# Sliding-window attention with a mixture of adapters: longer load runs, a new row order, and the copies that undo it

## The chip, the cores and the metric

The kernel runs on one core of one Trainium2 chip. The metric is the device time of one execution in microseconds (us). The core has five engines that run their own instruction queues in order: TensorE (PE, with its weight loads shown as PEld), VectorE (DVE), ScalarE (ACT), GpSimd (POOL) and SyncE (SP). Sixteen DMA engines move data; here POOL issues all loads and SP all stores.

## The reference

`q`, `k` and `v` have shape (8 batches, 8 heads, 576 positions, 64). Attention sees only keys within 32 positions:

```
scores = q @ k.T / sqrt(64), masked to |i - j| <= 32
attn   = softmax(scores);  x = (attn @ v), heads side by side: (4608, 512)
logits = x @ w_gate                    # 8 experts
w      = softmax over the two best experts
out    = x + sum over the two experts of w_e * (x @ A[e]) @ B[e]   # rank 16
```

Output is float32; the kernels compute in f16 with float32 accumulation.

## The kernel before

**Work units.** Two heads form a pair, so a batch has four pairs and the kernel 32 units `u` (`b, n = divmod(u, 4)`). The 576 keys of a unit are nine blocks of 64; both heads of a pair stand in one 128-row stationary operand (`kTs`, block diagonal), so one score matmul gives, for one key block, 128 rows (64 keys for each of two heads) by 128 query columns: the block's own 64 queries and 32 on either side. Eight blocks form a score tile `t` of two PSUM banks; 36 tiles run across the unit borders (4.5 tiles a batch).

**One unit.** `transposes(u, 0)` and `(u, 1)` turn q and k into `qTs` and `kTs` through a PSUM tile `tp` (pool `pt`, two buffers). `score(t)` first writes the mask with a matmul by `ident` (L182), then adds the scores (L186), and ScalarE's exponential writes them to one of four `PTs` (L191). `pv(u)` multiplies by `vbd` (L206), whose extra column of ones gives the row sums; VectorE takes the reciprocal (`rc`, L214) and scales into `xs` (`xb`, L215).

**The adapters.** One batch later, `moe_step` runs in four parts: `moe_xT` transposes `xs` (L227, L230; pool `pt` too) and `moe_zl` computes logits and all eight low-rank products (L238), a chain of small VectorE operations makes the gate, ending in `zs` (L262); `moe_zT` (L271, L274) and `moe_out` (L282, L284, L287) finish, two groups of 128 rows at a time, and SP stores (L291).

**Loads.** `load(b, w)` fetches q or k with two-row runs, three DMAs each, and `pair_heads` (L92) regroups heads on VectorE; `load_v` fetches v in sixteen DMAs of one-row runs. All go two batches ahead through POOL's queue, and cast from float32 to f16 on the way.

**Layout of rows.** Because two neighbouring positions share a partition (`j = 2`), queries and keys are held even positions first, and L187 of the kernel writes the score columns back in position order: `out=ps[:, i].rearrange("p (k j) -> p j k", j=2)`.

**Order.** The kernel's text gives an order by unit: regroup, transposes two units ahead, scores one unit ahead, the product, the adapter part of four units ago. The framework then orders the instructions on each engine at build time. PSUM tiles of `score`, `pv`, `moe_zl` and `moe_out` share one pool of three (`pw`).

Of the kernel before, what the change touches and what calls it, by code (L numbers as in the profile page):

```python
# [28 lines left out]
def kernel(  # L29
# [18 lines left out]
    NB = 9  # L48
    NG = 5
    TB = 8  # L50
    GS = 188
    VD = D + 1
    NEG = -30000.0
    NU = B * NP
    NT = NU * NB // TB

# [9 lines left out]


    NV = 3
    vbd = [const.tile([128, NP, NB, 2 * VD], F16, name=f"vbd{i}") for i in range(NV)]

    def load(b, w):
        d = load_pool.tile([96, 3, H, 2, D], F16, tag=f"l{w}", name=f"l{w}")
        src = (q, k)[w][b].rearrange("h (g p j) d -> g p h (j d)", g=3, j=2)
        for g in range(3):
            nc.gpsimd.dma_start(
                out=d[:, g].rearrange("p h j d -> p h (j d)"), in_=src[g])
        raw[b, w] = d

    def load_v(b):
        d = vbd[b % NV]  # L80
        src = v[b].rearrange("(n h) (a p j) d -> h j n p a d", h=2, p=32, j=2)
        for n in range(NP):
            for h in range(2):
                for j in range(2):
                    p0 = 64 * h + 32 * j
                    nc.gpsimd.dma_start(  # L86
                        out=d[p0:p0 + 32, n, :, VD * h:VD * h + D], in_=src[h, j, n])

    def pair_heads(b, w):
        d = cast_pool.tile([96, 3, 2, H, D], F16, tag=f"c{w}", name=f"c{w}")  # L90
        for g in range(3):
            nc.vector.tensor_copy(out=d[:, g],  # L92
                                  in_=raw[b, w][:, g].rearrange("p h j d -> p j h d"))
        qk[b, w] = d

    raw, qk = {}, {}
    load(0, 0)
    load(0, 1)

# [3 lines left out]
    for i in range(NV):  # L103
        nc.vector.memset(vbd[i], 0.0)
        nc.vector.memset(vbd[i][0:64, :, :, D], 1.0)
        nc.vector.memset(vbd[i][64:128, :, :, VD + D], 1.0)

    load_v(0)
    pair_heads(0, 0)
    pair_heads(0, 1)  # L110


    mask = const.tile([128, 4, 128], F16)
    nc.gpsimd.memset(mask, 0.0)
    for s in range(4):
        jk = s % 2
        blk = mask[32 * s:32 * s + 32]
        nc.gpsimd.affine_select(out=blk, in_=blk, compare_op=ALU.is_ge, fill=NEG,
                                base=-jk, channel_multiplier=-2,
                                pattern=[[0, 4], [1, 128]])  # L120
        nc.gpsimd.affine_select(out=blk, in_=blk, compare_op=ALU.is_ge, fill=NEG,  # L121
                                base=64 + jk, channel_multiplier=2,
                                pattern=[[0, 4], [-1, 128]])

    NQ = 4
    qTs = [const.tile([128, 2, 320], F16, name=f"qT{i}") for i in range(NQ)]
    kTs = [const.tile([128, NB, 128], F16, name=f"kT{i}") for i in range(NQ)]
    for t in qTs:
        nc.vector.memset(t[:, :, 0:16], 0.0)
        nc.vector.memset(t[:, :, 304:320], 0.0)  # L130
    for t in kTs:
        nc.vector.memset(t, 0.0)
    NPT = 4
    PTs = [const.tile([128, TB, 256], F16, name=f"PT{i}") for i in range(NPT)]
    for t in PTs:
        nc.vector.memset(t, 0.0)
# [3 lines left out]
    load_v(1)  # L140

# [13 lines left out]

    def transposes(u, which):
        b, n = divmod(u, NP)
        src = qk[b, which].rearrange("p g j h d -> p g j (h d)")
        tp = pt.tile([128, 1024], F16, tag="t", name="tp")
        for g in range(3):  # L160
            for j in range(2):
                if which == 0:
                    o = tp[:, 288 * j + 96 * g:288 * j + 96 * g + 96]
                else:
                    o = tp[:, 192 * g:192 * g + 192].rearrange(
                        "p (a j k) -> p a j k", a=3, j=2)[:, :, j]
                nc.tensor.matmul(  # L167
                    out=o, lhsT=src[:, g, j, 128 * n:128 * n + 128],
                    rhs=ident[0:96, 0:96], is_transpose=True, start=True, stop=True)
        if which == 0:  # L170
            nc.vector.tensor_copy(
                out=qTs[u % NQ][:, :, 16:304],
                in_=tp[:, 0:S].rearrange("p (j s) -> p j s", j=2))
        else:
            kt = tp[:, 0:S].rearrange("p (a k) -> p a k", k=64)
            nc.vector.tensor_copy(out=kTs[u % NQ][0:64, :, 0:64], in_=kt[0:64])  # L176
            nc.scalar.copy(out=kTs[u % NQ][64:128, :, 64:128], in_=kt[64:128])  # L177

    def score(t):
        ps = pw.tile([128, TB, 128], F32, tag="w", name="ps")  # L180
        for i in range(0, TB, 4):
            nc.tensor.matmul(out=ps[:, i:i + 4], lhsT=ident, rhs=mask,  # L182
                             start=True, stop=False)
        for i in range(TB):
            u, a = divmod(TB * t + i, NB)
            nc.tensor.matmul(  # L186
                out=ps[:, i].rearrange("p (k j) -> p j k", j=2),  # L187
                lhsT=kTs[u % NQ][:, a, :],
                rhs=qTs[u % NQ][:, :, 32 * a:32 * a + 64],
                start=False, stop=(i % 4 == 3))  # L190
        nc.scalar.activation(out=PTs[t % NPT][:, :, 64:192], in_=ps,  # L191
                             func=AF.Exp, scale=1.0 / float(D) ** 0.5)
# [3 lines left out]
    def pv(u):  # L196
# [4 lines left out]
        for g in range(NG):  # L201
            ops = [(a, off) for a, off in ((2 * g - 1, 128), (2 * g, 64), (2 * g + 1, 0))
                   if 0 <= a < NB]
            for i, (a, off) in enumerate(ops):
                t, sl = divmod(NB * u + a, TB)
                nc.tensor.matmul(  # L206
                    out=po[:, GS * g:GS * g + 2 * VD],
                    lhsT=PTs[t % NPT][:, sl, off:off + 128],
                    rhs=vbd[b % NV][:, n, a, :],
                    start=(i == 0), stop=(i == len(ops) - 1))  # L210
# [3 lines left out]
        nc.vector.reciprocal(out=rc, in_=pog[:, :, :, D])  # L214
        nc.vector.tensor_tensor(  # L215
            out=xs[b][:, :, 128 * n:128 * n + 128].rearrange("p g (h d) -> p g h d", h=2),
            in0=pog[:, :, :, 0:D], in1=bcast(rc, 3, D), op=ALU.mult)

# [58 lines left out]
    def moe_out(b, gs):  # L277
        zT = st[b, "zT"]
        n = len(gs)
        pd = pw.tile([128, 2, DD], F32, tag="w", name="pd")  # L280
        for i, g in enumerate(gs):
            nc.tensor.matmul(out=pd[:, i], lhsT=zT[:, g], rhs=B_sb,  # L282
                             start=True, stop=False)
            nc.tensor.matmul(out=pd[:, i], lhsT=ident, rhs=xs[b][:, g],  # L284
                             start=False, stop=True)
# [21 lines left out]

    for w in (0, 1):
        transposes(0, w)
    for w in (0, 1):  # L310
        transposes(1, w)
# [10 lines left out]
    for u in range(NU):  # L322
        b, n = divmod(u, NP)
        if n == 0 and b + 1 < B:
            pair_heads(b + 1, 0)
        if n == 1 and b + 1 < B:
            pair_heads(b + 1, 1)
# [4 lines left out]
        if u + 2 < NU:  # L332
            transposes(u + 2, 0)
            transposes(u + 2, 1)
# [40 lines left out]
```

## Time and profile before

| | |
|---|---|
| median of three runs | 215.91 us (215.25 to 219.85) |
| span of the profiled execution (core 0) | 211.4 us; no other time is recorded for it |
| mean granted TensorE clock | 0.936 |
| busy PE, DVE, ACT, POOL | 147.6, 119.9, 85.6, 128.3 us |
| instructions | 4124 |
| chain that ended last, by engine | PE 52%, DVE 19%, POOL 11%, ACT 9% |
| HBM read, written | 28.85 MB, 9.44 MB |
| DMA packets | 86642, of which 81888 under 512 B |

The span runs from the first to the last instruction. The page's slices divide it in 40 stretches of 5.3 us, each digit a busy share in tenths; its groups put together instructions of one line, engine and operands, with the idle time of the engine just before them and what ended it. In the list of waits the numbers are total us, count, longest. In the chain and the timeline each row is start, duration, engine, what. A mean over several pipelined matmuls overstates what one adds; the length of a run of them divided by their number does not.

### The profile page before, as it was taken

Reading aid. Unit: us, or ns where it says so; the run is one execution under the profiler, and the core shown is the slowest. Engines: PE = TensorE matmul, PEld = TensorE weight load, DVE = VectorE, ACT = ScalarE, POOL = GpSimd, SP = SyncE. Lnnn points to the kernel's source line nnn. Section 1 sums busy time; section 2 is a strip of 40 time slices with the busy share of each in tenths; the row PEclk is TensorE's granted clock in tenths of the full one; section 3 lists DMA queues with packets and bytes.
Section 4 is the critical chain, followed back from the end, with each engine's and each line's share of the span. In section 5 each row is a group of like instructions: output and inputs, shape, how many; then the busy total and the mean of one; then the engine's idle time right before and its main releaser. Section 6 shows DMA issues by size and latency. Waiting matters only on the chain.

```text
span 211.4 us, 4124 instructions
## 1 busy us (share of the span) xinstructions
PE 147.6 (70%) x1600; PEld 114.4 (54%) x1600; DVE 119.9 (57%) x337; ACT 85.6 (40%) x109; POOL 128.3 (61%) x197
## 2 busy tenths in 40 slices
PE   0030279998299949987699729964998599848481
PEld 0010158996268835876378626864687468726330
DVE  6787026668814891379346851688349734844700
ACT  2001015663357334553275144723683466246032
POOL 7999995999799469835983797699480000000000
PEclk9999999999969995999699997999999999999955
DMA  6998099999999998998999999999993023003306
GB/s 59 157 63 56 1 140 125 67 42 154 138 101 144 244 96 54 208 210 87 63 167 249 103 89 153 258 98 147 172 189 55 0 90 136 5 0 123 100 0 223
DMA packets 86642, 24.12 MB, mean 114 GB/s; under 512 B 81888, under 2 KB 82016, under 8 KB 86624
## 3 DMA queue, kind: packets, MB, share of 16 engines
q0 software_dynamic: 81376, 14.44, 86.3%
q1 hardware_dynamic: 5248, 9.44, 13.2%
q8 instruction: 12, 0.20, 0.4%
q14 instruction: 6, 0.05, 0.1%
HBM read 28.85 MB, written 9.44 MB: 181 GB/s over the span
## 4 chain that ended last, share of the span: by engine, by line
PE 52%; DVE 19%; POOL 11%; ACT 9%; issue 4%; DMA 3%; ACTq 0%; POOLq 0%
PE ps L186 13%; PE po L206 9%; PE ps L182 7%; PE pd L282 5%; PE tp L167 5%; PE pd L284 5%; POOL vbd_82 L86 4%; DVE xb L215 4%; PE pz L238 3%; DMA l_189<-in_k_dram 3%; DVE zs L262 3%; PE tx L227 3%; DVE xT L230 3%; ACT zT L274 3%; PE tz L271 2%
## 5 line engine op out<-in xcount | busy, mean ns | idle before, releaser
L86 POOL DMA_DIRECT2D vbd_83<-in_v_dram x48 | 29.3, 616 | 12.0 <-DMA vbd_83<-in_v_dram 4.8
L86 POOL DMA_DIRECT2D vbd_82<-in_v_dram x48 | 29.3, 617 | 9.0 <-DMA l_496<-in_q_dram 2.7
L182 PE MATMUL ps<-mask,ident 128*128 128x512 f16 x72 | 24.6, 423 | 12.7 <-POOL mask L121 12.0
L214 DVE RECIPROCAL rc<-po 128x10 f32<-128x10 f32 x32 | 7.0, 218 | 38.2 <-PE po L206 38.1
L287 ACT COPY obt<-pd 128x1024 f32<-128x1024 f32 (+1 forms) x24 | 20.8, 869 | 16.8 <-PE pd L284 16.0
L215 DVE TENSOR_TENSOR xb<-po,rc 128x640 f16<-128x640 f32 x32 | 26.2, 820 | 0.7
L86 POOL DMA_DIRECT2D vbd_84<-in_v_dram x32 | 19.5, 619 | 7.3 <-DMA vbd_84<-in_v_dram 2.6
L282 PE MATMUL pd<-B_sb,zT 128*128 128x512 f16 x40 | 18.3, 459 | 4.2 <-ACT zT L274 4.2
L271 PE MATMUL tz<-ident,zs 128*128 128x128 f16 x40 | 4.0, 234 | 21.0 <-DVE zs L262 21.0
L227 PE MATMUL tx<-ident,xb 128*128 128x128 f16 x160 | 14.7, 220 | 5.4 <-DVE xT L230 4.8
L284 PE MATMUL pd<-xb,ident 128*128 128x512 f16 x40 | 18.4, 461 | 0.0
L230 DVE COPY xT<-tx 128x512 f16<-128x512 f16 x40 | 15.6, 416 | 2.4 <-PE tx L227 1.6
L177 ACT COPY kT_164<-tp 64x576 f16<-64x576 f16 x8 | 5.1, 633 | 25.0 <-DVE kT_164 L176 25.0
L227 PEld LDWEIGHTS <-xb 128*128 128x128 f16 x160 | 11.3, 101 | 6.9 <-issue 4.9
L271 PEld LDWEIGHTS <-zs 128*128 128x128 f16 x40 | 2.4, 102 | 22.8 <-DVE zs L262 22.8
L182 PEld LDWEIGHTS <-ident 128*128 128x128 f16 x72 | 6.6, 110 | 14.3 <-issue 14.1
L238 PE MATMUL pz<-WA_sb,xT 128*128 128x136 f16 x160 | 13.9, 223 | 0.4 <-DVE xT L230 0.4
L186 PE MATMUL ps<-qT_160,kT_164 128*128 128x128 f16 x72 | 11.1, 317 | 2.4 <-ACT kT_164 L177 2.4
L177 ACT COPY kT_161<-tp 64x576 f16<-64x576 f16 x8 | 5.1, 634 | 18.2 <-DVE kT_161 L176 18.1
L274 ACT COPY zT<-tz 128x640 f16<-128x640 f16 x8 | 5.5, 692 | 16.6 <-PE tz L271 16.6
L191 ACT ACTIVATE PT_178<-ps 128x1024 f16<-128x1024 f32 x9 | 9.2, 1023 | 6.6 <-PE ps L186 5.7
L191 ACT ACTIVATE PT_180<-ps 128x1024 f16<-128x1024 f32 x9 | 9.2, 1023 | 6.1 <-PE ps L186 5.2
(209 smaller groups left out, 375.4 us busy)
## 6 DMA issues: line engine op xcount, KB each, us to landing
out_dram<-obt SPq DMA_DIRECT2D x24, 256.0 KB, 4.0
out_dram<-obt SPq DMA_DIRECT2D x16, 192.0 KB, 2.7
vbd_82<-in_v_dram POOLq DMA_DIRECT2D x48, 36.0 KB, 2.8
vbd_83<-in_v_dram POOLq DMA_DIRECT2D x48, 36.0 KB, 3.4
vbd_84<-in_v_dram POOLq DMA_DIRECT2D x32, 36.0 KB, 3.2
l_85<-in_q_dram POOLq DMA_DIRECT2D x3, 192.0 KB, 4.8
l_89<-in_k_dram POOLq DMA_DIRECT2D x3, 192.0 KB, 6.4
l_185<-in_q_dram POOLq DMA_DIRECT2D x3, 192.0 KB, 4.6
```

Of the source, the lines that this page charges most:

```text
L86: nc.gpsimd.dma_start(out=d[p0:p0 + 32, n, :, VD * h:VD * h + D], in_=src[h, j, n])
L182: nc.tensor.matmul(out=ps[:, i:i + 4], lhsT=ident, rhs=mask, start=True, stop=False)
L186: nc.tensor.matmul(out=ps[:, i].rearrange("p (k j) -> p j k", j=2), lhsT=kTs[u % NQ][:, a, :], rhs=qTs[u % NQ][:, :, 32 * a:32 * a + 64], ...
L191: nc.scalar.activation(out=PTs[t % NPT][:, :, 64:192], in_=ps, func=AF.Exp, scale=1.0 / float(D) ** 0.5)
L206: nc.tensor.matmul(out=po[:, GS * g:GS * g + 2 * VD], lhsT=PTs[t % NPT][:, sl, off:off + 128], rhs=vbd[b % NV][:, n, a, :], start=(i == 0) ...
L215: nc.vector.tensor_tensor(out=xs[b][:, :, 128 * n:128 * n + 128].rearrange("p g (h d) -> p g h d", h=2), in0=pog[:, :, :, 0:D], in1=bcast( ...
L227: nc.tensor.matmul(out=tp[:, 128 * c:128 * c + 128], lhsT=xs[b][:, g, 128 * c:128 * c + 128], rhs=ident, is_transpose=True, start=True, st ...
L230: nc.vector.tensor_copy(out=st[b, "xT"][:, g].rearrange("p c k -> p (c k)"), in_=tp[:, 0:512])
L238: nc.tensor.matmul(out=pz[:, GS * g:GS * g + ER + E], lhsT=xT[:, g, c, :], rhs=WA_sb[:, c, :], start=(c == 0), stop=(c == 3))
L282: nc.tensor.matmul(out=pd[:, i], lhsT=zT[:, g], rhs=B_sb, start=True, stop=False)
L284: nc.tensor.matmul(out=pd[:, i], lhsT=ident, rhs=xs[b][:, g], start=False, stop=True)
L287: nc.scalar.copy(out=ob[:, 0:n], in_=pd[:, 0:n])
```

## The change

- **Loads.** q and k come in runs of eight rows of one head, v in runs of two rows (eight DMAs). `load_v` puts both rows of a run side by side in `vbd`; `shift_v` then moves the second row to its own partitions with two VectorE copies. The head pairs are now heads `n` and `n + 4`.
- **Transposes.** A batch is transposed in three thirds of 96 partitions instead of by unit, 16 matmuls each third; `regroup` brings the two heads of a pair together first (two VectorE copies a third). `qTs` and `kTs` hold a whole batch, two buffers each. ScalarE writes all of q, undoing the eight-row order as it reads PSUM; VectorE and ScalarE write one half of k each.
- **Scores.** Query columns are now in position order, so score columns are written contiguously; only the keys are permuted.
- **Mask.** It becomes the stationary operand (`maskT`, 128 columns), the moving one is `ident` repeated four times.
- **Values.** The column of ones comes first, and the moving operand is two runs of 65.
- **Residual.** Added by four matmuls with the transposed x (`xT`) against `ident`, instead of one with `ident` against `xs`.
- **Setup.** Fewer zeros are written on VectorE; those for the second `kTs` and the second and third `vbd` go to POOL, behind the second batch's loads and ahead of the weights.

```diff
     def load(b, w):
-        d = load_pool.tile([96, 3, H, 2, D], F16, tag=f"l{w}", name=f"l{w}")
-        src = (q, k)[w][b].rearrange("h (g p j) d -> g p h (j d)", g=3, j=2)
+        d = load_pool.tile([FT, NT3, 2, J * D], F16, tag=f"l{w}", name=f"l{w}")
+        src = (q, k)[w][b].rearrange("(o n) (p j) d -> (n p) o (j d)", o=2, j=J)
...
     def load_v(b):
+        src = v[b].rearrange("(o n) (a p j two) d -> o j p (n a) (two d)",
+                             o=2, p=8, j=4, two=2)
+        for o in range(2):
+            for j in range(4):
+                p0 = 64 * o + 8 * j
+                c0 = VW * o + V0
+                nc.gpsimd.dma_start(out=d[p0:p0 + 8, :, c0:c0 + 2 * D], in_=src[o, j])
+
+    def shift_v(b):
+        d = vbd[b % NV]
+        for o in range(2):
+            p0 = 64 * o
+            c0 = VW * o + V0
+            nc.vector.tensor_copy(out=d[p0 + 32:p0 + 64, :, c0:c0 + D],
+                                  in_=d[p0:p0 + 32, :, c0 + D:c0 + 2 * D])
+
+    def regroup(b, t):
+        for w in (0, 1):
+            nc.vector.tensor_copy(
+                out=qk[b, w][:, t],
+                in_=raw[b, w][:, t].rearrange("p o (j d) -> p j o d", j=J))
...
+    maskT = const.tile([128, 2, 2, 4, 8], F16)
+    nc.gpsimd.memset(maskT, 0.0)
...
     load(1, 0)
     load(1, 1)
     load_v(1)
+    shift_v(0)
+    init_kq(1, nc.gpsimd)
+    init_v(1, nc.gpsimd)
+    init_v(2, nc.gpsimd)
...
+    def transposes(b, t):
+        for w in (0, 1):
+            src = qk[b, w].rearrange("p t j o d -> p t j (o d)")
+            tp = pt.tile([128, 1024], F16, tag="t", name="tp")
+            for j in range(J):
+                slot = j if w == 0 else 4 * (j % 2) + j // 2
                 nc.tensor.matmul(
+                    out=tp[:, FT * slot:FT * slot + FT], lhsT=src[:, t, j, :],
+                    rhs=ident[0:FT, 0:FT], is_transpose=True, start=True, stop=True)
+            if w == 0:
+                c0 = QP + J * FT * t
+                nc.scalar.copy(
+                    out=qTs[b % 2][:, c0:c0 + J * FT].rearrange("p (f j) -> p f j", j=J),
+                    in_=tp[:, 0:J * FT].rearrange("p (j f) -> p f j", j=J))
+            else:
+                kt = tp[:, 0:J * FT].rearrange("p (j a f) -> p a j f", j=J, f=8)
...
+                    if o == 0:
+                        nc.vector.tensor_copy(out=dst, in_=src_)
+                    else:
+                        nc.scalar.copy(out=dst, in_=src_)
...
-            nc.tensor.matmul(out=ps[:, i:i + 4], lhsT=ident, rhs=mask,
-                             start=True, stop=False)
+            nc.tensor.matmul(out=ps[:, i:i + 4],
+                             lhsT=maskT.rearrange("p o a j f -> p (o a j f)"),
+                             rhs=bcast(ident, 1, 4), start=True, stop=False)
...
-                out=ps[:, i].rearrange("p (k j) -> p j k", j=2),
-                lhsT=kTs[u % NQ][:, a, :],
-                rhs=qTs[u % NQ][:, :, 32 * a:32 * a + 64],
+                out=ps[:, i], lhsT=kTs[b % 2][:, NB * n + a, :],
+                rhs=qTs[b % 2][:, c0:c0 + 128],
...
-                    rhs=vbd[b % NV][:, n, a, :],
+                    rhs=rhs[:, :, V0 - 1:V0 + D],
...
-            nc.tensor.matmul(out=pd[:, i], lhsT=ident, rhs=xs[b][:, g],
-                             start=False, stop=True)
+            for c in range(4):
+                nc.tensor.matmul(out=pd[:, i, 128 * c:128 * c + 128], lhsT=xT[:, g, c],
+                                 rhs=ident, start=False, stop=(c == 3))
...
+        if n < 2 and b + 1 < B:
+            regroup(b + 1, n + 1)
+        if n == 2 and b + 1 < B:
+            shift_v(b + 1)
+        if n == 3 and b + 2 < B:
+            regroup(b + 2, 0)
+        if n < NT3 and b + 1 < B:
+            transposes(b + 1, n)
```

More of the change, by code (lines that the diff above doesn't have):

```diff
@@ L109 @@
[L109 to L123, printed above, removed]
```

134 lines of the change are left out of this document (63 added, 71 removed).

## The prediction, made before the changed kernel was run

> **What bounds the kernel now.** I read the page first: shares, the 40 slices, the DMA queues.
>
> ```profile
> span 211.4 us, 4124 instructions
> PE 147.6 (70%) x1600; PEld 114.4 (54%) x1600; DVE 119.9 (57%) x337; ACT 85.6 (40%) x109; POOL 128.3 (61%) x197
> ...
> PEclk9999999999969995999699997999999999999955
> DMA  6998099999999998998999999999993023003306
> ...
> q0 software_dynamic: 81376, 14.44, 86.3%
> ```
>
> The DMA engines look full for the first 160 us, which invites a prediction about transfers. The waits decide whether that counts:
>
> ```profile
> DVE rc L214 <- PE po L206: 38.1, 24, 4.4
> PE tz L271 <- DVE zs L262: 21.0, 8, 3.3
> PE ps L182 <- POOL mask L121: 12.0, 1, 12.0
> DVE c_275 L92 <- DMA l_185<-in_q_dram: 10.7, 3, 8.6
> ```
>
> The one long DMA wait of a compute engine (c_275) is at the start; later loads run two batches ahead and only POOL, which issues them, waits for landings. So DMA does not set the steady pace. What recurs is PE waiting for `zs` and VectorE waiting for PE. I therefore cut the batch in two stages, in two successive periods, at `zs` (gated z) and at the `rc` of the batch's fourth head pair (call it C):
>
> ```profile
> 124.67 0.82 DVE L262 TENSOR_TENSOR zs<-pz,gate 128x640 f16<-128x640 f32 x1
> 134.95 0.22 DVE L214 RECIPROCAL rc<-po 128x10 f32<-128x10 f32 x1 [1.50 <-PE po L206]
> 146.84 0.82 DVE L262 TENSOR_TENSOR zs<-pz,gate 128x640 f16<-128x640 f32 x1
> 157.08 0.22 DVE L214 RECIPROCAL rc<-po 128x10 f32<-128x10 f32 x1 [2.80 <-PE po L206]
> 164.01 0.20 DVE L248 TENSOR_REDUCE m_2246<-pz 128x5 f32<-128x40 f32 x1 [0.18 <-PE pz L238]
> 167.33 0.82 DVE L262 TENSOR_TENSOR zs<-pz,gate 128x640 f16<-128x640 f32 x1
> ```
>
> Stage 1, C to end of `zs` (the next batch's first pair D, x transposes, gate), took 12.7 and 11.1 us: VectorE's stage. Stage 2, end of `zs` to next C, took 9.5 and 9.4: PE's stage. The windows show the clock's part:
>
> ```profile
> core 0: us, PE busy (x) PEld busy (x) DVE busy (x) ACT busy (x) POOL busy (x), PEclk, DMA share, GB/s
> 57.00:79.00 22.00, 18.58 (x205) 14.39 (x205) 13.19 (x40) 11.16 (x14) 16.84 (x27) 0.91 1.26 142
> 125.50:147.70 22.20, 17.19 (x195) 13.46 (x195) 13.91 (x39) 9.98 (x13) 18.73 (x29) 0.92 1.46 164
> 147.70:168.20 20.50, 17.24 (x205) 13.89 (x205) 13.12 (x39) 11.16 (x14) 7.37 (x13) 1.00 0.86 109
> ```
>
> Periods whose granted clock was 0.91 and 0.92 took 22.0 and 22.2 us; the one at 1.00 took 20.5. Idle PE before `tz` and the following dip of PEclk go together.
>
> **The change, part by part.**
>
> ```profile
> 148.21 0.70 ACT zT L274
> ...
> 154.12 0.87 PE ps L186 x8
> 154.99 0.43 PE ps L182 x2
> 156.29 0.76 PE po L206 x13
> 163.98 0.47 PE tp L167 x11
> L92 DVE COPY c_1485<-l_1154 96x1024 f16<-96x1024 f16 x3 | 1.2, 414 | 0.0
> L104 DVE MEMSET vbd_82<- 128x2340 uint32 x1 | 2.0, 2008 | 1.3 <-PEq L359 1.3
> L176 DVE COPY kT_164<-tp 64x576 f16<-64x576 f16 x8 | 3.5, 439 | 0.0
> 180.49 2.21 DVE L230 COPY xT<-tx 128x512 f16<-128x512 f16 x5
> L215 DVE TENSOR_TENSOR xb<-po,rc 128x640 f16<-128x640 f32 x32 | 26.2, 820 | 0.7
> L177 ACT COPY kT_164<-tp 64x576 f16<-64x576 f16 x8 | 5.1, 633 | 25.0 <-DVE kT_164 L176 25.0
> L191 ACT ACTIVATE PT_179<-ps 128x1024 f16<-128x1024 f32 x9 | 9.2, 1023 | 4.7 <-PE ps L186 4.2 <-PE po L206 0.4
> L287 ACT COPY obt<-pd 128x1024 f32<-128x1024 f32 x16 | 16.2, 1012 | 16.3 <-PE pd L284 15.8 <-ACT PT_179 L191 0.5
> ```
>
> *Scores.* A score matmul costs 0.87/8 = 0.109 us, a value matmul of about as many columns, with contiguous output, 0.76/13 = 0.058. I take 0.058 (bounds 0.058 and 0.109): 36 a batch save 1.8 us of PE, a tile of 8 takes 0.46 instead of 0.87. The Trainium skill (Advanced Engine Details and Errata, PSUM Cachelines) says that non-contiguous PSUM access slows matmuls; the row agrees for today's every-second-word score output.
>
> *Mask, residual.* The mask matmul keeps 512 columns (0.43 for two). The residual becomes four 128-column matmuls, 0.23 us by the 0.058 row, for one of 0.21: nothing.
>
> *Transposes.* 48 a batch as before, 0.043 each (0.47/11). Their evacuation moves. ScalarE now takes q: its copies of 576 and the exponential of 1024 (633, 1023 ns) give 0.87 ns an element, so 768 elements cost 0.80 us. Three q and three half-k copies, 4.8 us a batch against 4 x 0.633 = 2.5. VectorE loses four q copies and keeps three half-k copies at 0.439 x 768/576 = 0.58 at most.
>
> *Shifts.* Two copies of 2304 f16 a batch. Scaling the 1024-element regroup gives 0.93; the memset of a like count took 2.01; one regroup, 0.41, is the floor. I take 0.85, since the regroup is the same kind of copy with a fixed part counted twice.
>
> *Loads.* Payload is unchanged, runs are two to four times longer; worth nothing in the steady part, since nothing on the path waits for them. If that cover were gone there would be no loss either, since packets only get fewer.
>
> *Stage 1 after.* The built order puts, on VectorE between C's `xb` and D's `rc`: both shifts, four of the six regroups. The two others stand around the first kT and xT. D's product waits for the shifts; behind them on VectorE queue D's `rc`, kT, xT, then PE's transposes and pz. Sum from C's `rc`: rc and xb 1.08, shifts 1.7, regroups 1.64, D's rc and xb 1.08, regroup 0.41, kT 0.54, xT 0.42, regroup 0.41, four xT at 0.44 (2.21/5) 1.77, last pz 0.3: 9.35 us against 164.01 - 157.08 = 6.9 in the undisturbed period. From there to end of `zs` took 4.1; after, the second kT stands inside the gate chain, and ScalarE has q 0.80 and k 0.80 queued ahead of the gate's exponential: +0.8. Stage 1: 14.2, against a mean of 11.9.
>
> *Stage 2 after.* end of `zs` to end of zT 1.25 (148.91 - 147.66), pd 0.89, transposes 0.36, mask and score 0.89, po 0.75, pd 0.89, mask and score 0.89, every second period another 0.89 (mean 0.45), po 0.75, latency 0.17: 7.3, where the same list with 0.109 scores gives 8.5. ScalarE's own list here (zT 0.70, q 0.80, k 0.80, two or three exponentials of 1.02, two output copies of 1.01) is 6.4 to 7.4: just hidden. Stage 1 now leaves PE two idle stretches of about 3 us (before xT, before tz), so I charge a clock dip in every period, 1.3: 8.6, against 9.45.
>
> A full period after is 14.2 + 8.6 = 22.8 us. The five full ones before (`zs` at 56.19, a row further down, to 167.33) average 22.2, dips included: +0.6 each, +3 in all.
>
> *Start.* POOL sets it.
>
> ```profile
> 24.20 0.63 POOL mask L121
> ...
> 56.19 0.74 DVE zs L262
> ...
> L86 POOL DMA_DIRECT2D vbd_83<-in_v_dram x48 | 29.3, 616 | 12.0 <-DMA vbd_83<-in_v_dram 4.8 <-DMA l_1816<-in_k_dram 1.7 <-PE tp L167 1.5
> L144 POOL DMA_DIRECT2D WA_sb<-in_moe_A_dram x4 | 3.5, 897 | 0.0
> L153 POOL DMA_DIRECT2D B_sb<-in_moe_B_dram x1 | 0.6, 586 | 0.0
> L114 POOL MEMSET mask<- 128x512 f16 x1 | 0.5, 543 | 0.0
> masks.py:199 POOL TENSOR_SCALAR_AFFINE_SELECT ident<-ident 128x128 f16<-128x128 f16 x1 | 2.9, 2926 | 0.1
> masks.py:197 POOL MEMSET ident<- 128x128 f16 x1 | 0.2, 223 | 0.0
> ```
>
> The mask follows 6 q and k issues (0.59 each, as B_sb's, which has a like number of pieces), 8 value issues at 0.62, half as many as now, and some 4 us of masks: ready at about 14 us instead of 24.8. But six memsets of some 2304 f16 move to POOL, at (543 - 223)/384 = 0.83 ns an element 2.1 us each, 12.6 in all, ahead of the weights and the third batch's loads. Adding POOL's queue (18 q and k issues, 16 value issues, masks 4, memsets 13.4 with the small ones, weights 4.9, from its start at 1.3) puts those loads' last issue near 44 us, landing near 47; VectorE's regroups of that batch stand in front of the first xT and wait for them. First `zs` ends near 55.5 instead of 56.9: -1.5. The 11 us won by the mask are spent in that wait.
>
> *Tail.* Last two periods, no regroups, fewer strided scores: -1.5.
>
> Sum: 211.4 + 3 - 1.5 - 1.5 = 211.4 us of span. No separate time is recorded for the profiled execution; the shown median of 215.9 stands 4.5 above its span, and I carry that: 216.
>
> **The rivals.**
>
> *Faster: PE is the bound.* PE's 70% and the 38.1 us of VectorE waiting for it speak for it. If shifts and regroups slip into VectorE's idle time (43% overall), stage 1 stays at 11.9, stage 2 falls to 7.3, a period to 19.2: five times -3.0, with start and tail -3: 193 of span, 198. Against: the idle time lies in stage 2, the added copies in stage 1.
>
> *Slower: ScalarE's q copies read PSUM with a 192-byte step.* A strided PSUM write made the score matmul 1.9 times dearer. If reads behave so, 0.80 becomes 1.44; ScalarE's stage 2 list then exceeds PE's (+0.64) and the gate waits another 0.3: +0.95 in seven periods, 222.5. It decides from about 1.1 us a copy. For: the rows have only contiguous ScalarE reads. Against: a ScalarE read need not share the matmul's limit. The section of the skill named above speaks of matmuls; its 8-byte line, taken for reads too, would give this result, and no run here shows it.
>
> *Slower: value matmuls pay.* Their moving operand becomes two 65-element runs at an odd offset. If today's score price came from its split moving operand instead of its output, 52 matmuls rise to 0.109, two products in stage 2 give +1.3 a period: 225. The same holds, at +1.2, if the scores stay at 0.109 (the change then misses what it says): 224; or shifts cost 2.0: +2.3 a period, 232.
>
> **How the numbers follow.** Forecast, balance within the 2% a measurement of this kernel can tell from no change: 0.38, 216 us, its own range 212 to 220. PE-bound and faster: 0.27. Strided q copies: 0.20. The remaining slower ones together: 0.15. Slower in all 0.35. The range runs from near the first rival's 198, whose full gain needs every VectorE copy hidden, hence 204, to 230, which takes in all slower prices but dear shifts.
>
> **What would show it.** Right: score pitch near 0.06 us; `zs` to C shorter by about 1, C to `zs` longer by about 2, VectorE without gaps between C and the first xT; first `zs` near 55 us after a VectorE wait for l of the third batch; PEclk dipping each period. Wrong: stage 1 no longer than 12 us, q copies at 1.1 us or more, value matmuls above 0.07, or POOL memsets below 1 us.

## The result, and the profile after

The changed kernel takes 229.18 us (median of four runs, 226.42 to 235.0) against 215.58 for the kernel before beside it (four runs, 213.79 to 219.85). It is slower: ratio 1.060, 95% interval 1.049 to 1.070. Ratios here compare undisturbed runs only and medians all runs, so the two can differ a little. The forecast was no change at 216, so the size was missed by 13 us. The profiled execution took 226.42 us, 2.1 more than its span of 224.3, so I compare spans below: 211.4 before, 211.4 forecast, 224.3 now.

From the page after, the shares, the granted clock, the DMA slices and the load queue:

```profile
span 224.3 us, 4265 instructions
PE 142.0 (63%) x1720; PEld 114.2 (51%) x1720; DVE 122.5 (55%) x305; ACT 102.4 (46%) x125; POOL 98.9 (44%) x139
...
PEclk9998599955879999796969999999699969997967
DMA  6999910999999999899925995790230023002306
...
q0 software_dynamic: 52704, 14.51, 85.2%
```

Every engine but ScalarE and VectorE does less than before, and the load queue has 35% fewer packets for the same bytes. Yet the span grew. The DMA slices read 1 and 0 in the sixth and seventh slice, 28 to 39 us, where those of the kernel before read 9, and PEclk falls to 5 in the ninth and tenth, 45 to 56 us. From the list of waits after (total us, count, longest):

```profile
DVE rc L246 <- PE po L238: 31.3, 18, 5.6
PE tz L302 <- DVE zs L293: 22.5, 8, 3.1
PE tp L187 <- DVE c L113: 11.2, 2, 8.4
DVE c L113 <- DMA l<-in_q_dram: 9.3, 4, 6.8
PE po L238 <- DVE vbd L108: 7.2, 5, 2.1
```

The first two are much as they were. New are TensorE waiting for the regrouped q and k of a later batch (8.4 us in one piece, up to 48.6; in the kernel before only its weight loads waited so, 9.6 us at the very start) and for the shifted v. VectorE waited long for a landing before, too (8.6 us), but for the second batch's, up to 28.7 us; the 6.8 us now are for the third's, up to 48.1. The same cut as in the prediction (C is the `rc` of a batch's fourth pair; stage 1 runs from C to the end of `zs`, stage 2 from there to the next C), read from VectorE's timeline of both kernels:

| us | before | after | forecast |
|---|---|---|---|
| end of the first `zs` | 56.92 | 63.16 | 55.5 |
| stage 1, mean of the five full periods | 12.05 | 14.36 | 14.2 |
| stage 2, mean of the five full periods | 10.20 | 8.76 | 8.6 |
| five full periods together | 111.23 | 115.60 | +3 |
| from there to the end | 43.25 | 45.54 | -1.5 |

The 12.9 us of span are thus 6.2 at the start, 4.4 in the five periods, 2.3 at the end. The windows of those five periods of the kernel after:

```profile
core 0: us, PE busy (x) PEld busy (x) DVE busy (x) ACT busy (x) POOL busy (x), PEclk, DMA share, GB/s
63.16:86.71 23.55, 17.28 (x220) 13.79 (x220) 13.77 (x37) 13.12 (x16) 15.61 (x24) 0.93 1.76 175
86.71:110.74 24.03, 17.86 (x210) 14.73 (x210) 13.74 (x37) 12.21 (x15) 11.75 (x17) 0.86 1.44 159
110.74:134.19 23.45, 17.29 (x220) 13.85 (x220) 13.74 (x37) 13.10 (x16) 10.21 (x14) 0.93 1.06 123
134.19:155.39 21.20, 14.92 (x210) 11.99 (x210) 13.72 (x37) 12.25 (x15) 6.41 (x8) 1.00 1.00 103
155.39:178.76 23.37, 17.30 (x220) 13.82 (x220) 13.47 (x37) 13.10 (x16) 0.00 (x0) 0.93 0.15 52
```

The last row has no loads at all and is no faster than the first, which had the queue full: transfers don't set this pace. Periods alternate between 220 and 210 matmuls (three score tiles in stage 2, or two), so a clock dip is priced only within one kind, as the experiments do below.

Where the start went is in the timelines of VectorE and of POOL (start, duration, what, idle before):

```profile
31.51 0.82 DVE L247 TENSOR_TENSOR xb<-po,rc 128x640 f16<-128x640 f32 x1
32.91 0.55 DVE L204 COPY kT<-tp 64x768 f16<-64x768 f16 x1 [0.57 <-PE tp L187]
...
34.98 4.18 DVE L108 COPY vbd<-vbd 32x2304 f16<-32x2304 f16 x2
...
48.10 0.42 DVE L113 COPY c<-l 96x1024 f16<-96x1024 f16 x1 [6.82 <-DMA l<-in_q_dram]
...
54.58 0.42 DVE L113 COPY c<-l 96x1024 f16<-96x1024 f16 x1 [0.61 <-DMA l<-in_k_dram]
...
62.34 0.82 DVE L293 TENSOR_TENSOR zs<-pz,gate 128x640 f16<-128x640 f32 x1
```

```profile
24.58 4.27 POOL L135 MEMSET kT<- 64x2304 f16 x2
...
29.03 4.19 POOL L135 MEMSET vbd<- 64x2340 f16 x2
...
33.84 4.71 POOL L135 MEMSET vbd<- 64x2340 f16 x2
...
44.25 1.97 POOL L89 DMA_DIRECT2D l<-in_q_dram  x3
46.15 1.94 POOL L89 DMA_DIRECT2D l<-in_k_dram  x3
```

POOL fills zeros from 24.6 us to 39.5 and only then issues the weights and the third batch's loads. VectorE gets the first of these at 48.1 and the last at 54.6, and the first batch's gate waits for its place behind them. The two shifts in the row of 4.18 us took 1.54 and 2.61.

### The profile page after: what moved, and what is told of

It reads as the page before. It is cut to its first block, busy times and chain, and to the rows that moved or that the text cites. A ratio compares the mean times of both kernels' runs of the same rounds, so it can differ in the third digit from the quotient of the medians.

```text
span 224.3 us, 4265 instructions
## 1 busy us (share of the span) xinstructions
PE 142.0 (63%) x1720; PEld 114.2 (51%) x1720; DVE 122.5 (55%) x305; ACT 102.4 (46%) x125; POOL 98.9 (44%) x139
## 3 DMA queue, kind: packets, MB, share of 16 engines
q0 software_dynamic: 52704, 14.51, 85.2%
## 4 chain that ended last, share of the span: by engine, by line
PE 33%; DVE 25%; POOL 14%; DMA 14%; issue 7%; ACT 5%; ACTq 0%; DVEq 0%; POOLq 0%
DMA l<-in_k_dram 9%; PE pz L269 5%; PE po L238 5%; PE tx L258 5%; POOL l L89 5%; PE ps L211 5%; DVE xb L247 4%; DVE vbd L108 4%; DVE c L113 4%; POOL vbd L135 4%; PE ps L218 4%; PE pd L313 4%; PE pd L316 3%; DMA vbd<-in_v_dram 3%; DVE zs L293 3%
## 5 line engine op out<-in xcount | busy, mean ns | idle before, releaser
L101 POOL DMA_DIRECT2D vbd<-in_v_dram x64 | 47.4, 747 | 40.3 <-PE po L238 30.3
L187 PE MATMUL tp<-ident,c 96*128 96x96 f16 x384 | 27.8, 228 | 29.8 <-POOL ident masks.py:199 12.8
L222 ACT ACTIVATE PT<-ps 128x1024 f16<-128x1024 f32 x36 | 36.4, 1024 | 13.9 <-PE ps L218 13.6
L187 PEld LDWEIGHTS <-c 96*128 96x128 f16 x384 | 23.3, 111 | 33.7 <-DVE c L113 19.6
L238 PE MATMUL po<-vbd,PT 128*128 128x130 f16 x416 | 32.3, 227 | 11.0 <-DVE vbd L108 7.2
L238 PEld LDWEIGHTS <-PT 128*128 128x128 f16 x416 | 27.1, 102 | 13.0 <-DVE vbd L108 8.1
L113 DVE COPY c<-l 96x1024 f16<-96x1024 f16 x48 | 20.3, 456 | 15.3 <-DMA l<-in_q_dram 9.3
L319 ACT COPY obt<-pd 128x1024 f32<-128x1024 f32 (+1 forms) x24 | 20.8, 870 | 14.2 <-PE pd L316 11.7
L211 PE MATMUL ps<-ident,maskT 128*128 128x512 f16 x72 | 27.0, 448 | 0.2
L218 PEld LDWEIGHTS <-kT 128*128 128x128 f16 x288 | 22.5, 110 | 8.5 <-issue 3.3
L218 PE MATMUL ps<-qT,kT 128*128 128x128 f16 x288 | 26.5, 242 | 0.0
L261 DVE COPY xT<-tx 128x512 f16<-128x512 f16 x40 | 16.4, 421 | 4.3 <-PE tx L258 2.3
```

The lines of the kernel that those rows point to most:

```text
L101: nc.gpsimd.dma_start(out=d[p0:p0 + 8, :, c0:c0 + 2 * D], in_=src[o, j])
L113: nc.vector.tensor_copy(out=qk[b, w][:, t], in_=raw[b, w][:, t].rearrange("p o (j d) -> p j o d", j=J))
L187: nc.tensor.matmul(out=tp[:, FT * slot:FT * slot + FT], lhsT=src[:, t, j, :], rhs=ident[0:FT, 0:FT], is_transpose=True, start=True, stop=True)
L211: nc.tensor.matmul(out=ps[:, i:i + 4], lhsT=maskT.rearrange("p o a j f -> p (o a j f)"), rhs=bcast(ident, 1, 4), start=True, stop=False)
L218: nc.tensor.matmul(out=ps[:, i], lhsT=kTs[b % 2][:, NB * n + a, :], rhs=qTs[b % 2][:, c0:c0 + 128], start=False, stop=(i % 4 == 3))
L238: nc.tensor.matmul(out=po[:, GS * g:GS * g + 2 * VD], lhsT=PTs[t % NPT][:, sl, off:off + 128], rhs=rhs[:, :, V0 - 1:V0 + D], start=(i == 0 ...
```

## Experiments: the start

Two things could make the fills dear: they stand ahead of the loads in POOL's queue, or they slow what VectorE does beside them (two shifts beside fills took 4.18 us). The first experiment moves the loads ahead of the fills of `vbd`.

```diff
-    init_kq(1, nc.gpsimd)
-    init_v(1, nc.gpsimd)
-    init_v(2, nc.gpsimd)
+    init_kq(1, nc.vector)
...
             load(b + 2, 0)
             load(b + 2, 1)
+            if u == 0:
+                init_v(1, nc.gpsimd)
+                init_v(2, nc.gpsimd)
```

> Edit: the third batch's q and k loads are issued before the zero fills of the second and third vbd on POOL, and the second kTs is zeroed on VectorE; nothing else. Theory 1 (the start is lost in POOL's queue, where 13 us of fills stand ahead of the weights and of the third batch's loads): these loads are issued at about 30 us instead of 44.3, VectorE's first regroup of that batch no longer waits, the first zs ends near 54 us instead of 63.2, later periods stay at 23 us, total about 220 us instead of 229. Rival (the loads are late because eight-partition value DMAs clog the DMA engines): the first zs moves by less than 3 us, total 226 or more.

Measured: 225.05 us (four runs, 220.48 to 226.12; the kernel before beside it 216.9), first `zs` at 62.57. The loads did land earlier, and the first `zs` came 0.6 us earlier, not 9. VectorE and POOL in that run:

```profile
40.99 3.54 DVE L108 COPY vbd<-vbd 32x2304 f16<-32x2304 f16 x2
44.56 5.99 DVE L113 COPY c<-l 96x1024 f16<-96x1024 f16 x5
```

```profile
38.90 4.21 POOL L135 MEMSET vbd<- 64x2340 f16 x2
...
44.78 4.55 POOL L135 MEMSET vbd<- 64x2340 f16 x2
```

The regroups no longer wait for data, but five of them now take 5.99 us together instead of some 2, because the fills run beside them: two took 2.38 each, the other three 0.4. The wait was turned into slow copies. (VectorE also zeroes the second `kTs` in this run, 2.4 us ahead of its first shifts.) So the theory missed. The rival's number for `zs`, less than 3 us, came true, but its reason did not, since the loads had landed. The second experiment takes this further in the queue: three load buffers, q and k of the third batch issued ahead of all fills.

```diff
-    load_pool = tc.alloc_tile_pool(name="load", bufs=2)
+    load_pool = tc.alloc_tile_pool(name="load", bufs=3)
...
     shift_v(0)
+    load(2, 0)
+    load(2, 1)
     init_kq(1, nc.gpsimd)
...
-        if n == 0 and b + 2 < B:
-            load(b + 2, 0)
-            load(b + 2, 1)
+        if n == 0 and b + 3 < B:
+            load(b + 3, 0)
+            load(b + 3, 1)
+        if n == 0 and b + 2 < B:
             load_v(b + 2)
```

> Edit of the changed kernel: q and k are loaded three batches ahead (three buffers). The same instructions, but the build then orders VectorE's work after C differently: kT, five xT and kT come first, shifts and regroups behind them. Theory 2: with the same VectorE work, C to end of zs falls from 14.1 to about 12.4 us because the gate starts earlier and both shifts stand behind the x transposes; and the third batch's loads come before the fills, so the first zs ends near 52 to 56 us: total 211 to 216. Rival (total VectorE work or DMA sets the period): the period stays at 23 us and only the start is won, 220 to 222.

Measured: 233.93 us (229.76 to 234.36; before 216.9), first `zs` at 63.84. Both theories missed. At the start it is the same story, five regroups in 7.81 us:

```profile
39.06 7.81 DVE L113 COPY c<-l 96x1024 f16<-96x1024 f16 x5
```

Its periods are longer too (24.09 us on average), and value matmuls wait for v, whose loads now stand behind more q and k. What share that wait has and what share the other order of VectorE's copies has, no run separates; this stays open.

The third takes the fills off POOL: ScalarE, which in the changed kernel makes its first copy at 13.6 us, copies them from one zero column (`zero_act` is a `nc.scalar.copy` with steps of zero). Only the narrow ones of 32 and 36 elements stay on POOL, those of the second `qTs` and `vbd` now ahead of the second batch's loads.

```diff
+    z1 = const.tile([128, 1], F16)
+    nc.vector.memset(z1, 0.0)
...
-        zero(eng, kTs[i][0:64, :, 64:128])
+        f = zero_act if i == 1 else (lambda ap, p0: zero(eng, ap))
+        f(kTs[i][0:64, :, 64:128], 0)
...
+    init_kq(1, nc.gpsimd)
+    init_v(1, nc.gpsimd)
     load(1, 0)
...
-    init_kq(1, nc.gpsimd)
-    init_v(1, nc.gpsimd)
     init_v(2, nc.gpsimd)
```

> The changed kernel with the six zero fills of kT1, vbd1 and vbd2 (11 us of GpSimd between 24.6 and 39.4 us) made by ScalarE in its idle first 15 us. Theory (GpSimd's fills cost the first batch its start twice over: they stand in the queue ahead of the third batch's loads, and VectorE's SBUF copies beside them take two to three times as long): the two shifts beside them fall from 4.18 to 1.7 us, the third batch's first regroup starts before 42 us instead of 48.1, the first zs ends at 55 to 57 us instead of 63.16, and the time is 220 to 224 us. Rival (the 16 transfer queues are full for the first 150 us, so the landings are late whatever GpSimd does): the first zs ends at 61 us or later and the time is 226 us or more.

Measured: 219.49 us (215.25 to 223.4; before 216.53; ratio to it 1.015, 0.982 to 1.048), first `zs` at 53.61, a little better than the theory. ScalarE's and VectorE's rows:

```profile
2.04 4.23 ACT L144 COPY kT<-z 64x2304 f16<-64x2304 f16 x2
6.28 8.72 ACT L144 COPY vbd<-z 64x2340 f16<-64x2340 f16 x4
```

```profile
38.10 1.58 DVE L108 COPY vbd<-vbd 32x2304 f16<-32x2304 f16 x2
...
41.93 1.90 DVE L113 COPY c<-l 96x1024 f16<-96x1024 f16 x5
...
52.79 0.82 DVE L304 TENSOR_TENSOR zs<-pz,gate 128x640 f16<-128x640 f32 x1
```

Shifts 0.79, regroups 0.38 each, no long wait. Of the 11.0 us of span that this takes off the changed kernel, 9.5 lie before the first `zs`. Read with the first two it is shown that the fills' place in the queue alone is not the price: whichever way the queue is ordered, either the data or the copies come late. This run removes both at once; how the gain divides between the two, no run separates.

The fourth asks what the shifts and the two-row runs of v are worth: v in sixteen one-row DMAs straight to its partitions, no shifts, on top of the first experiment.

```diff
-                nc.gpsimd.dma_start(out=d[p0:p0 + 8, :, c0:c0 + 2 * D], in_=src[o, j])
+                for e in range(2):
+                    p0 = 64 * o + 32 * e + 8 * j
+                    nc.gpsimd.dma_start(out=d[p0:p0 + 8, :, c0:c0 + D], in_=src[o, j, e])
```

> Edit on top of the first one: v is fetched in one-row runs, 16 DMAs a batch straight to the right partitions, and the two VectorE shifts are gone; the eight-row q and k runs stay. Theory 2 (VectorE's serial list from the batch's fourth pair C to zs sets the steady period, and the shifts are 1.6 us of it): C to end of zs falls from 14.1 to 12.5 us in every batch, the period from 23.0 to about 21.5; total some 8 to 10 us below the first edit alone, less 3 to 5 us at the start because POOL issues 16 more DMAs before the third batch's loads. Rival (DMA is the limit): the number of value pieces doubles, so the period does not fall or grows, total as the first edit or slower.

Measured: 233.23 us (230.17 to 234.36; before 216.9; ratio 1.085, 1.052 to 1.119). The total is the rival's, slower than the first experiment. From the list of DMA issues and from POOL's timeline:

```profile
vbd<-in_v_dram POOLq DMA_DIRECT2D x128, 36.0 KB, 7.1
```

```profile
48.37 1.97 POOL L89 DMA_DIRECT2D l<-in_q_dram  x3
```

The third batch's q is issued at 48.37 us instead of 34.30 in the first experiment, 14 us later. Some 11 of them are 16 more value loads that POOL issues ahead of it, at 0.67 us each; 3 are its waits for landings among these issues, 8.5 us in all instead of 5.5. Only the 3 can be laid to the DMA queue and its 90592 packets instead of 52704, the rival's reason. The first `zs` ends at 71.69, 9.1 us later than in the first experiment, and the next period is 27.24 us. Once the loads have caught up, the period is the theory's: the third and fourth full ones take 21.19 and 21.51 us, their way from C to the first gate operation 8.4 and 8.2 us against 9.3. So the 1.6 us of shifts are worth about 1.0 a period in stage 1, and having half as many value loads is worth more than that at the start.

## Experiments: the clock in every period

TensorE's wait for `zs` is followed by a stretch of 3.4 us at half clock in most periods. Here 32 transposes of `ident` into unread columns are put ahead of the `tz` transposes.

```diff
         tp = pt.tile([128, 1024], F16, tag="t", name="tz")
+        for g in range(32):
+            nc.tensor.matmul(out=tp[:, 640:768], lhsT=ident, rhs=ident,
+                             is_transpose=True, start=True, stop=True)
```

> The changed kernel with 32 more transposes of the identity on TensorE ahead of each batch's tz transposes, into columns of the same tile that nobody reads: 1.8 us of extra work at full clock, in the 2.76 us that TensorE waits for zs. Theory (that wait is what the half-clock stretch just behind it answers to, and the stretch costs some 2.2 us a batch: 23.45 us a period with one, 21.20 without): the 3.4 us stretches behind zs go, the five full periods add up to 106 to 109 us instead of 115.6, the first zs stays at 63 us, and the time is 218 to 221 us. Rival (the period is set by VectorE's stage 1, and what stage 2 gains is waited out there, or the extra work only delays tz): periods add up to 114 us or more, time 226 us or more.

Measured: 220.34 us (219.47 to 221.41; before 216.53; ratio 1.034, 1.021 to 1.046), the five periods together 106.77. (The first `zs` ends at 66.85, later than forecast, though what leads up to it is as in the changed kernel: POOL waited 5.4 us for landings ahead of its fills instead of 2.4, and the third batch's last k came 2.9 us later. So the start varies by some 3 us from one profiled execution to another; the three runs with the fills on ScalarE and the changed kernel's score columns have their first `zs` at 53.61, 54.46 and 56.31.) A window of that run:

```profile
88.24:108.81 20.57, 16.55 (x242) 13.78 (x242) 13.71 (x36) 12.21 (x16) 13.09 (x19) 1.00 1.61 180
```

The total came as expected, the price of a dip did not: the 2.2 us of the expectation compared a period of 220 matmuls with one of 210. Like with like, stage 2 of the longer kind takes 9.38 us with a dip, and 8.06 without (the run with fills on ScalarE, third full period); of the shorter kind 8.49 and 7.14. So a dip in stage 2 costs 1.3 us, what the prediction charged. (The one dip that fell into a stage 1, in the period that ends at 110.74, cost 1.5: 15.54 us against 14.07 in its neighbours.) The rest of the gain, 0.6 us a period, is the built order: eight transposes of the next q that stood behind `tz` now stand ahead of it, inside the wait. A run with 44 extra transposes instead of 32, on top of the fills on ScalarE, separates the two by chance, since there the eight went back behind `tz`:

```profile
120.86 2.62 PE L313 MATMUL tz<-ident 128*128 128x128 f16 x44
123.66 0.45 PE L316 MATMUL tz<-ident,zs 128*128 128x128 f16 x5 [0.19 <-DVE zs L304]
123.95 0.51 PE L198 MATMUL tp<-ident,c 96*128 96x96 f16 x8
```

> Fills on ScalarE and 44 instead of 32 extra transposes ahead of tz (2.5 us at 0.057 us each, in a wait of 2.76 us). Theory (TensorE's wait for zs is what brings the half clock, and with 32 a wait of 0.75 us a batch was left): 205 to 210 us, the first zs at 54 to 55 us, and five periods of 105 to 109 us. Rival (the extra transposes now reach past the end of zs, late by some 0.5 us in each of eight batches and by double that where the clock is at half): 212 us or more.

Measured: 212.59 us (six runs, 210.27 to 215.26; before 217.02; ratio 0.989, 0.976 to 1.002). The number is the rival's, its reason is not: the 44 end before `zs` does. Stage 2 is 8.02 to 8.06 and 7.14 us, the dip-free figures without the moved transposes.

Both edits together, 32 transposes and fills on ScalarE (no new lines of code):

> Both edits: fills on ScalarE and the 32 extra transposes ahead of tz. Theory (two separate losses, one at the start and one in every period): the first zs at 55 to 57 us, the five periods 106 to 109 us, time 210 to 216 us, that is at or below the kernel before. Rival (a shorter start only moves the loads of the batches into each other, or the gains are the same time counted twice): 218 us or more.

Measured: 209.05 us (204.64 to 210.31), below every run of the kernel before beside it (13 runs, median 216.53, 212.05 to 221.54); for this one no interval of a ratio is at hand. First `zs` 54.46, five periods 108.95, in its TensorE timeline:

```profile
139.16 1.95 PE L313 MATMUL tz<-ident 128*128 128x128 f16 x32
140.95 0.51 PE L198 MATMUL tp<-ident,c 96*128 96x96 f16 x8
142.09 0.45 PE L316 MATMUL tz<-ident,zs 128*128 128x128 f16 x5 [0.64 <-DVE zs L304]
```

The two losses add: against the changed kernel's median of 229.18 (on another chip run, whose kernel before took 215.58) -9.7 for the fills, -8.8 for the transposes, -20.1 for both. By spans the 16.4 us are 8.7 at the start, 6.7 in the periods, 1.1 at the end. This is the best version here. Something is left in it: in two of its five periods half-clock stretches fall into stage 1 (from 89.6 us for 3.4, from 110.1 for 6.8), which then takes 15.55 and 16.05 us instead of 14.07.

## Experiments: the score columns

The kernel before, with contiguous score columns and nothing else (this leaves out the return of the columns to position order, so mask and value matmuls meet them in another order; the amount of work is the same):

```diff
-                out=ps[:, i].rearrange("p (k j) -> p j k", j=2),
+                out=ps[:, i].rearrange("p (j k) -> p j k", j=2),
```

> The kernel before with one part of the change alone: score columns are written contiguously (the column order within a block is then not undone, so that part of the result differs). Theory: the score pitch falls from 0.109 to 0.058 us, the stage from end of zs to C (10.2 us on average) shortens by about 1 us, the other stage by little, total 207 to 210 instead of 215.6. Rival (the split moving operand makes the scores dear): the pitch stays at 0.109 and the time at 215. Second rival (PE's time there is cover for something else): pitch falls and the time stays within 2 us.

Measured: 212.45 us (ten runs, 210.47 to 215.15; before 216.9; ratio 0.995, 0.986 to 1.004): no change that can be told. The pitch did fall, at full clock to (155.82 - 155.38)/8 = 0.055 us:

```profile
155.38 0.61 PE L186 MATMUL ps<-qT,kT 128*128 128x128 f16 x8
155.82 0.59 PE L182 MATMUL ps<-mask,ident 128*128 128x512 f16 x2
```

Only the order of the output changed here, the moving operand is still in two runs, so the first rival falls and the price of 0.109 us is the output's. The second rival, that the time hardly moves, is nearest. Busy TensorE fell, and the clock fell with it:

```profile
57.91:79.93 22.02, 18.16 (x205) 13.71 (x205) 13.44 (x41) 10.94 (x14) 17.13 (x27) 0.85 1.27 142
...
147.87:168.59 20.72, 17.02 (x205) 13.01 (x205) 13.18 (x40) 10.94 (x14) 12.25 (x20) 0.92 1.22 143
```

These two periods had 0.91 and 1.00 in the kernel before, and half clock in all five adds up to 27 us instead of 17. To see whether the clock ate the gain, the 32 transposes were added to this kernel and, for comparison, to the kernel before itself (the edit as above).

> The kernel before with contiguous score columns alone (212.45 us) and the 32 extra transposes ahead of tz. Theory (the 14.7 us that the contiguous columns take off TensorE came back as half-clock stretches, 44.9 us in all against 29.4 in the kernel before): fewer of them, and 204 to 208 us. Rival (the score part was hidden behind VectorE in stage 1, and the clock has no part in it): 211 us or more.

> The kernel before with the 32 extra transposes ahead of tz. Theory (the half clock behind the wait for zs costs the kernel before too, 3 to 4 stretches of 3.4 us in five periods and 12.4 us at the end): 211 to 214 us. Rival (what TensorE does earlier in stage 2 is waited out in stage 1): within 1 us of the kernel before, 215 to 217 us.

Measured: 211.4 us (210.89 to 212.6; before 216.53; ratio 0.992, 0.986 to 0.997) and 213.55 us (211.75 to 215.11; before 217.02; ratio 1.003, 0.996 to 1.010). The medians are 5.1 and 3.5 us below those of the kernel before, but only the first ratio's interval stays below 1. The 204 to 208 us expected of the first did not come; its time is its rival's. The second lies in its theory's 211 to 214 us by its median, but by the ratio no change can be told. The build scattered the extra transposes over the order in these two kernels. The first still had 30 us at half clock, 17 of them in its five periods, as many as the kernel before. In the second 3.4 us were left in the periods, and these add up to 107.77 us instead of 111.23. So without the half clock the kernel before gains some 3.5 us of its span in the periods; that the clock alone ate the gain from the contiguous columns is not shown.

In the changed kernel it can be asked the other way round: the version of 209.05 us with every second column again.

```diff
-                out=ps[:, i], lhsT=kTs[b % 2][:, NB * n + a, :],
-                rhs=qTs[b % 2][:, c0:c0 + 128],
+                out=ps[:, i].rearrange("p (k j) -> p j k", j=2),
+                lhsT=kTs[b % 2][:, NB * n + a, :],
+                rhs=qTs[b % 2][:, c0:c0 + 128].rearrange("p (k j) -> p j k", j=2),
```

> Fills on ScalarE, 32 extra transposes, and the score columns strided again (every second column of the score tile, the query read in the same steps), the rest as in the changed kernel. Theory (0.109 instead of 0.057 us for each of 288 score matmuls, that is 15 us of TensorE, of which the two thirds in stage 2 lie on the path): 216 to 221 us, stage 2 at 8.2 to 9 us instead of 7.04 and stage 1 as it was, 14 to 15 us. Rival (the pitch is hidden behind ScalarE's exponentials, and the columns' order is worth nothing): within 2 us of 209.

Measured: 216.48 us (214.92 to 218.36; before 217.02; ratio 1.012, 0.997 to 1.027), 7.4 above the version of 209.05. TensorE's timeline and a window:

```profile
147.35 1.04 PE L229 MATMUL ps<-qT,kT 128*128 128x128 f16 x8
148.19 0.95 PE L250 MATMUL po<-vbd,PT 128*128 128x130 f16 x13
```

```profile
78.93:100.41 21.48, 18.40 (x242) 15.41 (x242) 13.72 (x37) 12.28 (x16) 10.22 (x14) 1.00 1.39 149
```

Eight scores take 0.84 us to the start of the next group, against 0.45 contiguous. At full clock stage 2 is 8.74 and 7.42 us where the version of 209.05 has 7.40 and 6.51: +1.3 with three tiles in it, +0.9 with two, the full price. Stage 1 stays at 14.07 in the four periods without half clock in it: there the price is hidden. Theory right.

## Why the prediction was right or wrong

**Stages: right.** Stage 1 was forecast at 14.2 and measured at 14.36, of which 0.3 is the one dip in it (four of the five are at 14.0 to 14.2). Stage 2 was forecast at 8.6 and measured at 8.76, and there two errors cancel by luck: its list was put at 7.3 without a dip and is 7.7 (8.06 in the three longer ones, 7.14 in the two shorter, as measured without a dip), and the dip charged to every period came in four of five. (The prediction's 9.45 for stage 2 before is the mean of two periods; over the five it is 10.20.) The rows behind them, from the changed kernel's groups:

```profile
L192 ACT COPY qT<-tp 128x768 f16<-128x768 f16 x24 | 19.2, 799 | 44.3 <-PE tp L187 44.3
L108 DVE COPY vbd<-vbd 32x2304 f16<-32x2304 f16 x16 | 15.1, 944 | 0.5
```

and from its TensorE timeline:

```profile
137.15 0.61 PE L218 MATMUL ps<-qT,kT 128*128 128x128 f16 x8
137.60 0.91 PE L238 MATMUL po<-vbd,PT 128*128 128x130 f16 x13
138.34 0.38 PE L313 MATMUL pd<-B_sb,zT 128*128 128x512 f16 x1
```

q copies 0.80 as forecast, so the rival of the strided reads falls; scores 0.056 and value matmuls 0.057 (0.45/8, 0.74/13), so the rivals of the split operand and of scores that stay dear fall; a shift in the periods 0.79 against 0.85 (the group's 0.94 includes those beside fills). A dip was charged with 1.3 and costs 1.3. The rival in which TensorE is the bound falls, since stage 1 did not stay at 11.9.

**Five periods: right in sign, near in size.** +4.4 against +3: a period came to 23.12 us where 22.8 was forecast. Half-clock stretches within the five periods add up to 17 us in either kernel, so there is no more of them than before; that each costs the same in both is not shown.

**Start: the step that failed.** The sum put the last issue of the third batch's loads near 44 us, landing near 47, first `zs` at 55.5, -1.5. Measured: the last of these issues ends at 48.1, the last landing is at 54.6, `zs` at 63.16, +6.2. From the last landing to `zs` the forecast had 8.5 us and the run has 8.6. So the whole miss of this execution, 7.7 us at `zs`, was already there at the landing: about 4 us in POOL's list and 3.5 in the transfer.

- In POOL's list, POOL's own waits for landings ahead of the fills, 2.4 us, were put at nothing, and the fills took 14.9 us instead of 13.4. (Issues were 2.6 dearer and the masks 2.6 cheaper than charged.)
- The landing was charged with 3 us, from no row. The last third of k was there 6.5 us after the issues had ended (the first third of q, issued from 44.25, at 48.1). The kernel before already showed more than 3 in its list of DMA issues, whose last number is the median us from issue to landing:

```profile
l_185<-in_q_dram POOLq DMA_DIRECT2D x3, 192.0 KB, 4.6
l_189<-in_k_dram POOLq DMA_DIRECT2D x3, 192.0 KB, 6.7
```

That a fill and a VectorE copy between SBUF tiles stand in each other's way the sum did not have at all. In the changed kernel itself this adds little: the slow shifts end at 39.2 us, and VectorE then waits for the landing all the same. But it decides what a repair is worth: with loads early and the fills beside the copies 0.6 us are won, no more than the start varies by itself; with the fills on another engine 6.9 to 9.5. The rival "shifts cost 2.0 us" was thus true of the one pair that met fills, and only of it.

**Tail: failed.** -1.5 forecast, +2.3 measured, of which the last period is 1.3 (14.47 against 13.13 us) and the one before it 0.9. Its stage 2 is 7.27 us with a half-clock stretch from 201.4, and 6.04 before without one. That difference of 1.2 is about the price of one dip, but no run separates it. In the period before, 0.7 of the 0.9 is in stage 1, where the shifts still stand and no regroup does. The gain from the scores was not seen there.

**Wrong place for the loads.** "Worth nothing in the steady part" holds (the period without loads is no faster), but at the start it matters how many value loads POOL has to issue, as the run with one-row v shows.

**The carry.** The 4.5 us between span and median was no property of the kernel: the profiled execution after took 2.1 more than its span.

**The range.** 229.18 lies just inside the outer range of 204 to 230 us, and that is luck: the upper end was set by the prices of slower rivals (strided q copies, dear value matmuls, scores that stay dear), none of which came true. The time came from the start, which the forecast had as a gain.

## What to carry to other kernels

Work that is moved to an idle engine has to be placed in time, not only in share: ask what stands behind it in that engine's queue, and which instructions of the neighbouring engine run in the same microseconds. Ask how long the loads of the kernel before took to land, before charging a landing. A faster TensorE stage that ends in the same wait may hand part of its gain back through the clock (argued here, not shown), so price a dip between periods of the same make-up, and try filling the wait with work that is already due before filling it with work that is not.

## What the runs showed of the hardware

- A VectorE copy from SBUF to SBUF beside a POOL fill took 0.8 to 2.7 us, taken one by one, instead of 0.4 (regroup) or 0.8 (shift). In the changed kernel fills ran from 33.84 to 35.91 and from 35.95 to 38.55 us, the two shifts from 34.98 to 36.52 and from 36.55 to 39.16: each shift ends 0.6 behind a fill, and the second fill took 2.60 instead of 2.07. Instructions that read PSUM did not slow: `xb` 0.82 and kT 0.55 us beside the fills that begin at 29.03. The Trainium skill (SBUF — State Buffer, "SBUF: two separate sides") describes a port pair that GpSimd and certain VectorE instructions share, where whichever starts first blocks the other for the whole instruction; the traces agree.
- In four of the five full periods a TensorE wait of 2.76 us for `zs` was followed by a half-clock stretch of 3.4 us, in one (134.19 to 155.39) by none. With 32 transposes in the wait no stretch followed `zs` in the five periods. The Trainium skill (TensorE: Matmul & The Clock Gate, "HAM oscillation") puts the limit at gaps above some 3.4 us; here shorter ones, among other small gaps, were enough.
- A two-part moving operand of 65 columns each, at an odd offset, costs nothing (0.057 us against 0.058 for 130 columns in one run). An every-second-column f32 output nearly doubles a score matmul: 0.109 against 0.055 us in the kernel before, where nothing but the output's order changed, and 0.105 against 0.056 in the changed kernel, where the moving operand was read in the same steps.
